# A tuned attention and SwiGLU kernel: units 12 to 15 by 15 products per three feature blocks, and silu as one activation

## Chip, cores and metric

The kernel runs on one core of a Trainium2 chip. Times are device microseconds of that core; the metric is the median of repeated executions. The core has a matmul engine (TensorE, "PE" in the profile, with its weight loads as "PEld"), VectorE (DVE), ScalarE (ACT), GpSimd (POOL) and a queue that issues transfers (SP). Each runs its own instructions in order, and semaphores tie them together.

## What is computed

Two stages, cut from the reference. The attention output of all tokens (4 batches of 768, 8 heads of 48) is reshaped to 3072 rows of 384 and goes through a gated feed-forward block with 1536 features:

```python
for t in range(S):
    cur = np.einsum('bhd,bhe->bhde', u[None] * kt, vt)
    y[:, :, t] = np.einsum('bhd,bhde->bhe', rt, state + cur)
    state = w[None, :, :, None] * state + np.einsum('bhd,bhe->bhde', kt, vt)
...
g = x @ w_gate
silu = g * (1.0 / (1.0 + np.exp(-g)))
val = x @ w_val
return (silu * val @ w_out)
```

## The kernel before

**Tiling.** Tokens are cut into 24 units of 128 (6 chunks of 4 batches). Attention makes, for unit i, a transposed input tile xT (384 rows in three blocks of 128, by 128 tokens). The feed-forward block works on groups g of two units (256 tokens), and from g = 2 on two groups at a time. Its 1536 features are 12 blocks of 128; each needs gate and value. All is fp32, so one 128x256 product shows as two matmul records in the profile.

**Three forms of the same products.** A plain group (`gate_value`, L444, units 0 to 3) takes 3 products for the gate and 3 for the value of a feature block. For a pair of groups (512 tokens) `four` (L590, units 4 to 15) makes a block's gate and value from 11 products in place of 12, with sums of weights made by POOL (`w_sums`, L576) and of inputs made by VectorE (`x_sums`). The names p1 to p7, c11 to c22 are its products; `PLACE` (L556) says at which step each is issued, and ACT and VectorE copy and add the partial sums out of two PSUM chains, a and b. Copies p1, u2 and u3 go to partial buffers (a ring of six). For units 16 to 23 `three_units` (L808) takes three feature blocks at once: 15 rounds r0 to r14 of two products each (gate and value), in six PSUM chains (n, y, l4, l5, l1, l2, l8), for 30 products in place of 33. The weight forms that they need are made by POOL, six sums in place (`in_place`, L707) and nine into side buffers (`w_forms`, L719), the input forms by VectorE (`x_forms`, L751, 11 operations).

**Silu.** ACT makes the sigmoid into a buffer; VectorE (or POOL) multiplies it by the gate, then by the value.

**Projection.** `project` (L501) makes a group's output rows from seven products of quarter matrices, with sums from `h_sums` (L486), ACT copies and VectorE additions. `two_projections` (L663) gives the order in which two groups' items run ("00 10 01 02 11 04 03 12 05 06 13 14 15 16": group, product), and hangs the preparation of the next pair onto them.

**PSUM.** Eight banks: four for attention (also used by `three_units`), two for gate_value and chain a, one each for the tags "o" and "w_mag".

**Order.** The order is written out by hand. Step s of the main loop prepares unit s+1 (POOL scales k and r, L301 and L304), runs scores of s-1 (L381), outputs and update of s-2 (L411, L426), turns blocks of unit s on VectorE (L373) and moves those of s+1 by 16 transfers on SP (L358). Between these parts `gaps` (L907) calls `feed`, which takes feed-forward pieces from the list `todo`; `queue(g)` (L886) fills it at every second step with the 26 pieces of `four_units` for one pair and the projection items of the pair before. When the attention is done, the pieces of `three_units` run for units 16 to 23 with their projections.

Of the kernel before, what the change touches and what calls it, by code (L numbers as in the profile page):

```python
# [22 lines left out]
def fast(  # L23
# [39 lines left out]
    six = ctx.enter_context(tc.tile_pool(name="six", bufs=6))  # L63
    ps_a = ctx.enter_context(tc.tile_pool(name="ps_a", bufs=4, space=bass.MemoryType.PSUM))
    ps_w = ctx.enter_context(tc.tile_pool(name="ps_w", bufs=1, space=bass.MemoryType.PSUM))
    ps_f = ctx.enter_context(tc.tile_pool(name="ps_f", bufs=2, space=bass.MemoryType.PSUM))
    ps_o = ctx.enter_context(tc.tile_pool(name="ps_o", bufs=1, space=bass.MemoryType.PSUM))
# [18 lines left out]
    hTs = cst.tile([P, 2, FC, 2 * P], FP32, name="hTs")  # L86
# [81 lines left out]
    def round_high(n, half, bank):  # L168
        hi = halves(bits[n][:, :, 1], n)[half]
        ps, tag = ((ps_w, "w_mag"), (ps_o, "o"))[bank]  # L170
        mag = ps.tile([P, WN // 2], INT32, name="w_mag", tag=tag)
        mags[n, half] = mag[:].rearrange("p (c f) -> p c f", c=hi.shape[1])
        act.activation(
            mags[n, half].bitcast(FP32), hi.bitcast(FP32), AF.Copy, scale=float(2.0**-112)
        )
# [82 lines left out]
    act.activation(sg0[:], ident[:, 0:1], AF.Sigmoid)  # L258
# [185 lines left out]
    def gate_value(g, f):  # L444
        gv = ps_f.tile([P, 2, 2 * P], FP32, name="gv", tag="gv")
        for o, wt in enumerate((wg, wv)):
            for c in range(CC):
                pe.matmul(  # L448
                    gv[:, o, :].rearrange("p (i t) -> p i t", i=2),
                    wt[:, c, P * f : P * (f + 1)], xT[:, 2 * g % NX : 2 * g % NX + 2, c, :],  # L450
                    start=(c == 0), stop=(c == CC - 1),
                )
        sg = three.tile([P, 2 * P], FP32, name="sg", tag="sg")
        act.activation(sg[:], gv[:, 0, :], AF.Sigmoid)
        dve.tensor_mul(sg[:], sg[:], gv[:, 0, :])
        dve.tensor_mul(hT[g][:, f, :], sg[:], gv[:, 1, :])
# [44 lines left out]
    def project(g, n):  # L501

        h11, h12, h21, h22 = h_quarters(g)
        x = part_of.setdefault(g, {})
        if n == 0:
            one_bank = ps_f.tile([P, 2, 2 * P], FP32, name="o_f", tag="gv")[:, 0, 0:NH]
            if g % 2 == 0:
                x["a"] = ps_o.tile([P, 2 * P], FP32, name="o_a", tag="o")[:, 0:NH]
                x["b"] = one_bank
            else:  # L510
                x["a"] = one_bank
                x["b"] = ps_w.tile([P, 2 * P], FP32, name="o_b", tag="w_mag")[:, 0:NH]
            x["out"] = [two.tile([P, DM], FP32, name=n, tag=n) for n in ("o_sb1", "o_sb2")]
        lhs, rhs, acc = (
            (h11, w11, "a"), (h12, w21, "b"), (1, wt[0], "a"), (2, wt[1], "a"),
            (0, w12, "b"), (h22, wt[2], "a"), (3, w22, "b"),
        )[n]
        if isinstance(lhs, int):
            lhs = x["s"][lhs]
        ps = x[acc]  # L520
        for f in range(FH):
            pe.matmul(  # L522
                ps, lhs[:, f, :], rhs[:, f, :],
                start=(f == 0 and n in (0, 1, 4)), stop=(f == FH - 1), skip_group_check=True,
            )
        o1, o2 = x["out"]
        if n in (0, 2, 3):
            nm = {0: "p1", 2: "u2", 3: "u3"}[n]
            x[nm] = six.tile([P, 2 * P], FP32, name=nm, tag="part")[:, 0:NH]
            act.copy(x[nm], ps)  # L530
        elif n == 1:
            dve.tensor_add(o1[:, 0:NH], x["p1"], ps)
        elif n == 5:
            act.copy(o2[:, 0:NH], ps)
        elif n == 6:
            dve.tensor_add(o1[:, NH:DM], x["u2"], ps)  # L536
        if n in (3, 4):
            if "c22" in x:
                dve.tensor_add(o2[:, NH:DM], x["u3"], x["b"])
            x["c22"] = True  # L540
        if n >= 5:
            j = 6 - n
            c, b = divmod(2 * g + j, B)
            n0 = S * b + P * c
            act.dma_start(out=out[n0 : n0 + P, :], in_=x["out"][j][:])
# [44 lines left out]
    def four(g, f, what):  # L590

        x = part_of[g]
        if what == "p1":
            x["a", f] = ps_f.tile([P, 2, 2 * P], FP32, name="c_a", tag="gv")[:, 0]
        elif what == "p2":
            pool_of, tag = ((ps_o, "o"), (ps_w, "w_mag"))[f % 2]
            x["b", f] = pool_of.tile([P, 2 * P], FP32, name="c_b", tag=tag)[:]
        h = [hT[g + j][:, f, :] for j in range(2)]
        if what in ("sg0", "sg1"):
            j = int(what[2])  # L600
            x[what, f] = three.tile([P, 2 * P], FP32, name="sg", tag="sg")
            act.activation(x[what, f][:], h[j], AF.Sigmoid)  # L602
            return
        if what == "h1":
            dve.tensor_mul(h[1], h[1], x.pop(("sg1", f))[:])  # L605
            pool.tensor_mul(h[1], h[1], x.pop(("u3", f))[:])  # L606
            return
# [13 lines left out]
        ps = x[acc, f]  # L621
# [4 lines left out]
        if what in ("p1", "p6", "p7"):  # L626
            nm = {"p1": "p1", "p6": "u2", "p7": "u3"}[what]
            x[nm, f] = six.tile([P, 2 * P], FP32, name=nm, tag="part")
            act.copy(x[nm, f][:], ps)  # L629
        elif what == "c11":  # L630
            dve.tensor_add(h[0], x.pop(("p1", f))[:], ps)  # L631
        elif what == "c21":
            dve.tensor_mul(h[0], h[0], x.pop(("sg0", f))[:])
            dve.tensor_mul(h[0], h[0], ps)
        elif what == "c22":
            dve.tensor_add(x["u3", f][:], x["u3", f][:], ps)  # L636
        elif what == "c12":
            dve.tensor_add(h[1], x.pop(("u2", f))[:], ps)

    def four_units(g):  # L640

        steps = sorted((11 * f - 5 + at, f, what) for f in range(FC) for what, at in PLACE.items())
        if g + 2 == THREES:
            steps += [
                (11 * f + 20 + 5.4 * m, f, do)
                for f in (2, 5, 8) for m, do in enumerate(in_place(f // 3))
            ]
            steps.sort(key=lambda x: x[0])
# [14 lines left out]
    def two_projections(g):  # L663

        def item(j, p):
            if g >= THREES and (j, p) == (0, 1):
# [6 lines left out]
            elif g + 2 < THREES:  # L673
# [4 lines left out]
            if THREES <= g + 2 < N // 2:  # L678
# [6 lines left out]
    THREES = 8  # L685
# [33 lines left out]
    def w_forms(t):  # L719

        f = 3 * t
        made = wide["u", t] = {}

        w = [[wgv[:, :, c, P * (f + i) : P * (f + i + 1)] for c in range(CC)] for i in range(3)]
        def place():
            if t == 0:
# [24 lines left out]
    def x_forms(g):  # L751
# [4 lines left out]
        v += [  # L756
            t[:].rearrange("p h d -> p (h d)")[:, 0 : 2 * P].rearrange("p (i t) -> p i t", i=2)
            for t in r_ld + k_ld
        ]
        last = two.tile([P, H, D], FP32, name="xf", tag="rk")  # L760
        v.append(
            last[:].rearrange("p h d -> p (h d)")[:, 0 : 2 * P].rearrange("p (i t) -> p i t", i=2)
        )
        v10, v14, v6, v13, v2, v12, d1, v3, v1, v8, v4 = v
        dve.tensor_add(v10, x01, x21)
        dve.tensor_add(v14, x10, x20)
# [8 lines left out]
        dve.tensor_sub(v4, x01, x00)  # L775
        wide["v", g] = {
# [4 lines left out]
    def prepare_threes(g, n):  # L781
        if g > THREES:
            if n == 10:
                x_forms(g)
            return
        if n == 1:
            todo_forms.extend(in_place(3) + w_forms(1))
        if n == 7:
            todo_forms.extendleft(reversed(w_forms(0)))
# [4 lines left out]
    def three_step(g, t, n):  # L794

        what, chain = ROUNDS[27 - n if t == 3 and n > 12 else n]
        first = n == [c for _, c in ROUNDS].index(chain)
        if first:
            pool_of, tag = {"l4": (ps_o, "o"), "l2": (ps_w, "w_mag")}.get(chain, (ps_a, "a"))
            wide[chain] = pool_of.tile([P, 2, 2 * P], FP32, name=f"c_{chain}", tag=tag)  # L800
        u, v = wide["u", t][what], wide["v", g][what]
        for o in range(2):
            pe.matmul(  # L803
                wide[chain][:, o].rearrange("p (i t) -> p i t", i=2), u[:, o], v,
                start=first and o == 0, stop=True, skip_group_check=True,
            )

    def three_units(g):  # L808
# [8 lines left out]
        def bank(chain):  # L817
            return wide[chain][:].rearrange("p o t -> p (o t)")
# [4 lines left out]
        def silu(at, n, which, h, on, muls):  # L823
            sg = room["sg"][n].rearrange("p (j t) -> p j t", j=2)
            gate, value = (which[:, :, o] for o in range(2))
            todo.append((at, lambda: act.activation(sg, gate, AF.Sigmoid)))  # L826
            todo.append((muls, lambda: on.tensor_mul(sg, sg, gate)))  # L827
            todo.append((muls + 0.1, lambda: on.tensor_mul(h, sg, value)))

        if g == THREES:  # L830
            forms = w_forms(2) + w_forms(3)
            todo += [(2.1 * n + 0.2, do) for n, do in enumerate(forms)]
        for t in range(4):
            z = 15 * t
            for n in range(15):
                todo.append((z + n, lambda t=t, n=n: three_step(g, t, n)))
# [6 lines left out]
            later(z + 6.5, dve.tensor_sub, c[4], q14, "l4")  # L843
            later(z + 8.5, act.copy, x, "n")
# [9 lines left out]
            later(z + r0, dve.tensor_sub, c[2], c[2], "l2")  # L854
            later(z + 11.6, dve.tensor_sub, c[0], r12, "n")
# [30 lines left out]
    def queue(g):  # L886
# [5 lines left out]
        elif g % 2 and g > 1:  # L892
# [5 lines left out]
            *pieces, last = four_units(g - 1)  # L898
# [111 lines left out]
    for s in range(4, N + 2):  # L1010
# [34 lines left out]
        if s == 24:  # L1045
            x_forms(THREES)
# [434 lines left out]
```

## Time and profile before

| | |
|---|---|
| median of 3 runs | 618.14 us (617.55 to 618.4) |
| profiled execution | 618.37 us, its span 616.6 us |
| granted TensorE clock | 0.999 |
| TensorE busy | 601.6 us, 98% of the span |
| VectorE, ACT, POOL busy | 395.5, 235.0, 325.4 us |
| units 12 to 15 beside attention | about 343 to 418 us of the span |
| units 16 to 23 | from 450.5 us on |

The span is from the first to the last instruction; the execution's own time has some 1.8 us around it. A group's row names line, engine, operation and tiles (out<-in), then count, busy time, mean duration, and the engine's idle time ahead of the group with what ended it. A matmul's end is modelled and matmuls overlap in the pipeline, so their starts are read, not their durations. Idle time of an engine that sets nothing costs nothing.

### The profile page before, as it was taken

What the parts mean: (1) busy time and instruction counts of PE and PEld (TensorE: products, weight loads), DVE (VectorE), ACT (ScalarE), POOL (GpSimd) and SP (SyncE); (2) the same over time, 40 slices, a digit from 0 to 9 for tenths busy, and PEclk for the clock granted to TensorE, in tenths of its full rate; (3) what the DMA queues carried; (4) which work ended last, traced back from release to release, by engine and by line L of the source; (5) the groups of instructions that cost most, each with busy time, mean ns of one, the idle gap of its engine ahead of it and who ended that gap; (6) DMA issues with size and microseconds to landing.
All of it is one profiled execution on the core that took longest, in us unless ns stands there. A gap on an engine that the chain in (4) does not pass through costs nothing.

```text
span 616.6 us, 12802 instructions
## 1 busy us (share of the span) xinstructions
PE 601.6 (98%) x4992; PEld 541.4 (88%) x4992; DVE 395.5 (64%) x749; ACT 235.0 (38%) x599; POOL 325.4 (53%) x366
## 2 busy tenths in 40 slices
PE   8799999999999999999999999999999999999996
PEld 7588888899888899988899988889978889988896
DVE  6878997464556564466659255649268885478770
ACT  3368886321343422244431334442223331133310
POOL 4789789944638422764624747959736510012200
PEclk9999999999999999999999999999999999999999
DMA  7979982342331213323231503031000000100001
GB/s 176 224 208 244 245 289 46 65 69 59 73 66 25 33 22 71 70 32 55 43 48 29 112 13 48 11 48 28 27 27 2 0 1 14 38 1 2 1 2 55
DMA packets 138005, 40.44 MB, mean 66 GB/s; under 512 B 128592, under 2 KB 131792, under 8 KB 137936
## 3 DMA queue, kind: packets, MB, share of 16 engines
q1 hardware_dynamic: 134480, 34.82, 26.6%
q10 hardware_dynamic: 3456, 4.72, 2.1%
q8 instruction: 41, 0.67, 0.5%
q14 instruction: 28, 0.23, 0.1%
HBM read 28.51 MB, written 4.72 MB: 54 GB/s over the span
## 4 chain that ended last, share of the span: by engine, by line
PE 83%; DMA 4%; SPq 3%; POOL 3%; DVE 3%; ACT 2%; issue 1%; ACTq 0%; DVEq 0%; POOLq 0%
PE o_f L522 13%; PE c_b L622 11%; PE c_l L803 10%; PE c_a L622 10%; PE gv L448 8%; PE o_a L522 8%; PE o_b L522 6%; PE y_ps L411 5%; PE c_y L803 3%; PE c_n L803 3%; PE s_ps L381 3%; SPq L358 3%; DMA w_bits<-in_moe_w_gate_dram 1%; DMA w_bits<-in_moe_w_val_dram 1%; PE u_ps L426 1%
## 5 line engine op out<-in xcount | busy, mean ns | idle before, releaser
L448 PE MATMUL gv<-xT,wgv 128*128 128x256 f32 x288 | 66.8, 385 | 0.6 <-ACT xT L415 0.6
L322 ACT ACTIVATE At<-ident,du 128x128 f32<-128x128 f32 x176 | 61.0, 397 | 15.8 <-DVE o_sb L536 7.2
L622 PE MATMUL c_b<-xT,wgv 128*128 128x256 f32 x216 | 64.4, 380 | 0.0
L827 POOL TENSOR_TENSOR At<-At,hats 128x512 f32<-128x512 f32 x8 | 10.2, 1274 | 97.8 <-ACT At L826 97.8
L448 PEld LDWEIGHTS gv<-xT,wgv 128*128 128x128 f32 x288 | 53.2, 190 | 8.9 <-ACT xT L415 0.9
L606 POOL TENSOR_TENSOR hTs<-hTs,u 128x256 f32<-128x256 f32 x36 | 28.5, 791 | 48.6 <-DVE hTs L605 48.4
L622 PEld LDWEIGHTS c_b<-xT,wgv 128*128 128x128 f32 x216 | 40.7, 190 | 5.3
L629 ACT COPY u<-c_a 128x256 f32<-128x256 f32 x72 | 26.7, 371 | 47.8 <-PE c_a L622 44.9
L386 DVE COPY_PREDICATED At<-mask,s_ps 128x512 f32<-128x512 int32 x48 | 33.0, 742 | 18.2 <-PE s_ps L381 9.7
L622 PE MATMUL c_a<-t,s 128*128 128x256 f32 x144 | 43.6, 384 | 0.7 <-ACT p L629 0.7
L622 PE MATMUL c_a<-xT,wgv 128*128 128x256 f32 x144 | 42.8, 379 | 0.0
L602 ACT ACTIVATE sg<-hTs 128x256 f32<-128x256 f32 x72 | 29.9, 416 | 28.8 <-DVE hTs L631 21.1
L304 POOL TENSOR_TENSOR hats<-r_ld,scales 128x384 f32<-128x384 f32 x20 | 21.2, 1061 | 33.0 <-DMA hats<-hats 33.0
L622 PE MATMUL c_b<-xT,s 128*128 128x256 f32 x144 | 37.0, 379 | 0.0
L636 DVE TENSOR_TENSOR u<-u,c_b 128x256 f32<-128x256 f32 x36 | 15.0, 417 | 33.3 <-PE c_b L622 29.6
L411 PE MATMUL y_ps<-At,v_ld 128*32 128x128 f32 x768 | 34.9, 273 | 1.4 <-DVE At L386 1.4
L411 PEld LDWEIGHTS y_ps<-At,v_ld 128*32 128x32 f32 x768 | 30.3, 110 | 2.4 <-issue 1.4
L622 PEld LDWEIGHTS c_a<-t,s 128*128 128x128 f32 x144 | 26.7, 190 | 5.1 <-ACT p L629 1.5
L622 PEld LDWEIGHTS c_b<-xT,s 128*128 128x128 f32 x144 | 27.2, 190 | 3.9
L622 PEld LDWEIGHTS c_a<-xT,wgv 128*128 128x128 f32 x144 | 27.3, 190 | 3.6
L439 POOL TENSOR_TENSOR Z<-Z,w 48x192 f32<-48x192 f32 x32 | 18.7, 583 | 22.2 <-DVE Z L438 21.0
L411 PE MATMUL y_ps<-rT,Z 112*32 112x128 f32 x480 | 29.8, 276 | 0.5 <-ACT kT L347 0.5
(240 smaller groups left out, 1524.0 us busy)
## 6 DMA issues: line engine op xcount, KB each, us to landing
hats<-hats SPq DMA_DIRECT2D x192, 32.0 KB, 2.0
w_bits<-in_moe_w_gate_dram SPq DMA_DIRECT2D x6, 768.0 KB, 6.2
v_ld<-in_v_dram SPq DMA_DIRECT2D x48, 96.0 KB, 3.3
w_bits<-in_moe_w_val_dram SPq DMA_DIRECT2D x6, 768.0 KB, 6.6
w_bits<-in_moe_w_out_dram SPq DMA_DIRECT2D x6, 768.0 KB, 6.6
out_dram<-o_sb ACTq DMA_DIRECT2D x24, 192.0 KB, 2.0
k_ld<-in_k_dram SPq DMA_DIRECT2D x20, 192.0 KB, 3.1
r_ld<-in_r_dram SPq DMA_DIRECT2D x20, 192.0 KB, 4.2
```

Of the source, the lines that this page charges most:

```text
L304: pool.tensor_mul(rhat_of(i)[:, :, 0:D], raw(i)[1], rscale)
L322: lambda h=h: act.activation(At[i % 2][:, h, :], ident[:], AF.Identity, scale=du[:, h : h + 1])
L386: dve.copy_predicated(At[i % 2][:].rearrange("p (a e) t -> p a e t", e=2)[:, :, e], mask[:].bitcast(INT32).unsqueeze(1).to_broadcast([P, H ...
L411: pe.matmul(ps[32 * q : 32 * q + 32, cc, :], *x, start=start, stop=stop, skip_group_check=True,)
L439: pool.tensor_mul(ze, ze, w)
L448: pe.matmul(gv[:, o, :].rearrange("p (i t) -> p i t", i=2), wt[:, c, P * f : P * (f + 1)], xT[:, 2 * g % NX : 2 * g % NX + 2, c, :], start ...
L522: pe.matmul(ps, lhs[:, f, :], rhs[:, f, :], start=(f == 0 and n in (0, 1, 4)), stop=(f == FH - 1), skip_group_check=True,)
L602: act.activation(x[what, f][:], h[j], AF.Sigmoid)
L606: pool.tensor_mul(h[1], h[1], x.pop(("u3", f))[:])
L622: pe.matmul(ps.rearrange("p (i t) -> p i t", i=2), lhs, rhs, start=first, stop=what not in ("p2", "p5", "p4", "p3"), skip_group_check=True,)
L629: act.copy(x[nm, f][:], ps)
L803: pe.matmul(wide[chain][:, o].rearrange("p (i t) -> p i t", i=2), u[:, o], v, start=first and o == 0, stop=True, skip_group_check=True,)
```

## The change

Units 12 to 15 (g = 6 and 7) are made by a new function `three_beside`, with the 15 rounds of `three_units`, while attention still runs. It has four PSUM banks in place of six chains' own tiles, so its rounds stand in another order (`BESIDE`, and `ENDING` for the last three blocks), and a bank goes back to a list as soon as its last reader is issued. The four banks that were three pools are now one list, `take()` and `free`, for all feed-forward work. Silu is one ACT activation, in place where it can be; the product with the gate goes away everywhere. Partial buffers come from the list `free_part`, and projections keep partial sums in the output tiles. `in_place` for the first nine blocks moves from beside units 12 to 15 to beside units 8 to 11. `x_forms` for units 16 to 19 moves from the end of step 24 to ahead of a projection item of units 12 to 15 (item "13": group 7, product 3).

```diff
+    banks = [ps_f.tile([P, 4 * P], FP32, name=f"bank{n}") for n in range(4)]
+    free = deque(banks[:2])
+    def take():
+        return free.popleft()
...
     def gate_value(g, f):
-        gv = ps_f.tile([P, 2, 2 * P], FP32, name="gv", tag="gv")
+        bank = take()
+        gv = bank[:].rearrange("p (o t) -> p o t", o=2)
...
-        act.activation(sg[:], gv[:, 0, :], AF.Sigmoid)
-        dve.tensor_mul(sg[:], sg[:], gv[:, 0, :])
-        dve.tensor_mul(hT[g][:, f, :], sg[:], gv[:, 1, :])
+        sg = free_sg.popleft()
+        act.activation(sg, gv[:, 0, :], AF.Silu)
+        dve.tensor_mul(hT[g][:, f, :], sg, gv[:, 1, :])
+        free_sg.append(sg)
+        free.append(bank)
...
     def project(g, n):
+            x["a"] = take()
...
+        if n == 1:
+            x["b"] = take()
...
         elif n == 5:
             act.copy(o2[:, 0:NH], ps)
+            free.append(x["a"])
...
     def four(g, f, what):
         if what in ("sg0", "sg1"):
-            act.activation(x[what, f][:], h[j], AF.Sigmoid)
+            act.activation(h[j], h[j], AF.Silu)
...
         if what in ("p1", "p6", "p7"):
-            x[nm, f] = six.tile([P, 2 * P], FP32, name=nm, tag="part")
-            act.copy(x[nm, f][:], ps)
+            x[nm, f] = free_part.popleft()
+            act.copy(x[nm, f], ps)
         elif what == "c11":
-            dve.tensor_add(h[0], x.pop(("p1", f))[:], ps)
+            free_part.appendleft(x.pop(("p1", f)))
+            dve.tensor_add(h[0], free_part[0], ps)
         elif what == "c21":
-            dve.tensor_mul(h[0], h[0], x.pop(("sg0", f))[:])
             dve.tensor_mul(h[0], h[0], ps)
+            free.append(x["a", f])
...
-    THREES = 8
+    FIRST, THREES = 6, 8
...
+    BESIDE = (
+        ("r10", "n"), ("r14", "y"), ("r12", "l4"), ("r13", "n"), ("r2", "y"), ("r9", "l4"),
+        ("r5", "n"), ("r11", "y"), ("r6", "l5"), ("r3", "l1"), ("r1", "l2"), ("r7", "l5"),
+        ("r4", "l1"), ("r0", "l2"), ("r8", "l8"),
+    )
...
+    def three_beside(g):
+        for t in range(4):
+            z = 15 * t
+            rounds = ENDING if t == 3 else BESIDE
...
+            if t < 3:
+                forms = w_forms(g, t + 1)
...
+            later(at["r10"], act.copy, c[5], "n")
+            later(at["r14"], act.copy, c[4], "y")
+            later(at["r12"], act.copy, c[0], "l4")
+            later(at["r13"], dve.tensor_add, c[4], c[4], "n")
+            later(at["r2"], dve.tensor_add, c[5], c[5], "y")
+            later(at["r9"], dve.tensor_sub, c[4], c[4], "l4")
+            give(at["r9"] + 0.1, "l4")
+            later(at["r5"], act.copy, c[1], "n")
+            later(at["r5"] + 0.1, dve.tensor_sub, c[0], c[0], "n")
+            give(at["r5"] + 0.2, "n")
+            later(at["r11"], act.copy, c[2], "y")
+            later(at["r11"] + 0.1, act.copy, c[3], "y")
+            give(at["r11"] + 0.2, "y")
...
+            later(at["r8"], dve.tensor_sub, c[1], c[1], "l8")
+            later(at["r8"] + 0.1, dve.tensor_add, c[3], c[3], "l8")
+            give(at["r8"] + 0.2, "l8")
+            if t < 3:
+                for i, on in enumerate((dve, dve, pool)):
+                    silu(
+                        *((z + 11.7, z + 11.8) if i == 2 else (z + 15.6 + i / 10, z + 16.2 + i / 10)),
+                        hTs[:, :, 3 * t + i], values[:, :, i], on,
+                    )
...
-            *pieces, last = four_units(g - 1)
+            *pieces, last = (four_units if g - 1 < FIRST else three_beside)(g - 1)
...
-        if s == 24:
-            x_forms(THREES)
```

Here `later(at, ...)` places an operation after the round that stands at that place, and `c` are six pairs of a gate row in hTs and a value buffer, all 128x512: c0 to c5 are the gate and value of three feature blocks for both groups.

## Prediction, made before the changed kernel ran

> **What bounds the kernel now.** I read the page's busy times first, then its chain of waits, then TensorE's instructions in order of time. From the page:
>
> ```profile
> span 616.6 us, 12802 instructions
> PE 601.6 (98%) x4992; PEld 541.4 (88%) x4992; DVE 395.5 (64%) x749; ACT 235.0 (38%) x599; POOL 325.4 (53%) x366
> PE 83%; DMA 4%; SPq 3%; POOL 3%; DVE 3%; ACT 2%; issue 1%; ACTq 0%; DVEq 0%; POOLq 0%
> L622 PE MATMUL c_b<-xT,wgv 128*128 128x256 f32 x216 | 64.4, 380 | 0.0
> ```
>
> TensorE is busy for 98% and carries 83% of the chain. Matmuls overlap in the records (380 ns each), so a product must be priced by its distance to the next one. TensorE in order of time, in the stage that changes (units 12 to 15), with columns start, duration, what, and the wait ahead of it:
>
> ```profile
> 350.70 0.59 PE L622 MATMUL c_b<-t,s 128*128 128x256 f32 x2
> 351.13 0.59 PE L622 MATMUL c_b<-xT,wgv 128*128 128x256 f32 x2
> 351.57 0.59 PE L622 MATMUL c_a<-xT,wgv 128*128 128x256 f32 x2
> 352.26 0.70 PE L622 MATMUL c_a<-t,wgv 128*128 128x256 f32 x2
> 352.80 0.59 PE L622 MATMUL c_a<-xT,wgv 128*128 128x256 f32 x2
> ```
>
> A product is two records (x2), and products start 0.432 us apart: nothing but their number sets the pace here. At 352.26 one is late by 0.26 us, and the next by another 0.11: a wait costs its length and some 0.11 for the restart. Two other places show such waits, at 303.41 and at the start of units 16 to 19:
>
> ```profile
> 303.41 0.70 PE L622 MATMUL c_a<-t,s 128*128 128x256 f32 x2 [0.38 <-ACT p L629]
> ...
> 452.35 1.03 PE L803 MATMUL c_l<-xf,wgv 128*128 128x256 f32 x4
> 454.47 1.10 PE L803 MATMUL c_l<-xf,wgv 128*128 128x256 f32 x4 [1.09 <-DVE xf L771]
> 455.41 1.03 PE L803 MATMUL c_n<-xf,s 128*128 128x256 f32 x4
> ```
>
> The stage's own windows row shows what is left on the other engines (us, busy us of PE, weight load, DVE, ACT, POOL):
>
> ```profile
> 343.00:418.00 75.00, 74.90 (x596) 66.02 (x595) 41.56 (x92) 31.54 (x90) 53.01 (x70) 1.00 0.24 42
> ```
>
> **What the Trainium skill says.** "ScalarE: Activation LUTs", Step-by-step: every function takes one element per cycle and lane, 0.833 ns each. The trace agrees: the sigmoid of 128x512 took 630 ns and the copy 587, so I price silu as sigmoid. The same page, Table sets, has a 2.66 us switch between sets, and puts copies into every set; the trace has one table load of 1.28 us, at 0.80 us, and the changed program also has one on its path, so I charge none. "SBUF — State Buffer", Who interferes with whom: a VectorE instruction with two SBUF inputs contends with GpSimd's reads, one with a PSUM input doesn't. The trace agrees: L633 (two SBUF inputs) took 653 ns in this stage where L634 (one in PSUM) took 422. So new additions from PSUM keep their price and new products of SBUF tiles may take more.
>
> **Part by part.** (1) Products. `four` is 11 per feature block: L622 has 792 records over three pairs, 132 products for a pair. The 15-product form is 15 rounds of 2 for three blocks: L803 has 480 records over two pairs, 120 for a pair. So 12 fewer x 0.432 = **-5.18 us**, all on TensorE, which is the path. Attention, projections and DMAs keep their counts; no queue gets or loses a transfer.
>
> (2) Waits that exist now. `x_forms(8)` moves from behind step 24 to ahead of projection item 13 of units 12 to 15. Its 11 subtractions (0.42 each, 4.6 us) then lie beside three more items of 1.95 us and attention: the wait at 454.47 goes, 452.35 to 454.47 being 2.12 instead of 0.86, with 0.08 at the restart: **-1.33**. Next late there would be POOL's forms for round r13, of which POOL has six in-place sums fewer (6 x 0.74) in that stretch. The wait at 352.26 goes with `four`: **-0.37**. The wait at 303.41 (0.64 with its restart) and one at 188.79 to 191.24 (0.91, the same line) came from `p1`'s copy queueing for a buffer that POOL's product L606 held. Partial buffers are now taken from the side last released, so `p1` takes one that VectorE gave back and the wait for POOL falls on the copy four products later. I count two thirds of 1.55: **-1.0**.
>
> (3) Silu. It takes the product of a gate with its sigmoid away 96 times (24 in `gate_value`, 48 in `four` for units 4 to 11, 24 in units 16 to 23, 8 of them on POOL), some 0.4 to 0.7 us each. TensorE waits for none of them in the views above, so: 0, hidden by TensorE's own stream; if that cover were gone it would be a gain.
>
> (4) POOL and ACT. The in-place weight sums of units 12 to 15 (18 x 0.74 = 13 us) move up beside units 8 to 11, where POOL is busy 44.2 of 78.0 us: it fits, and this mix with `four` ran at 53 of 75 here. In the changed stage POOL loses some 16 in-place sums, 28 L584-588 sums and 10 L606 (about 42 us) and gains 27 forms and three products of 1.27 (24 us). ACT has 24 copies of 0.587 and 11 silus, 21 us against 23. Each is covered by a 70 us stage: 0. Bounds: -0.5 to +1.0.
>
> (5) New waits in the stage. VectorE gets, for three blocks, 12 additions from PSUM at 0.686 (the L821 row) and two products, 9.6 us beside 15 rounds of 0.864 = 13.0; attention adds 4.1 us a unit (two L386, two transposes, a reduction, two L438) while TensorE's part of it takes 3.1 (390.30 to 393.41). It fits on average, not everywhere. A handover TensorE to ACT or VectorE takes 0.20 to 0.37 in units 16 to 19 (round start 472.69, copy 472.89), back 0.15 (454.32 to 454.47). With four banks and these, the written order gives four late places:
> - Third round (r12) takes the bank that projection item 15 has just left: 0.20 + copy 0.32 + 0.15 = 0.67 late. Behind it on TensorE is item 16, then everything.
> - First change of block, counted from its round r10 at 0: r8 is in c1 and c3 at 1.6; ACT does the n copy, two silus, then the y copy to 3.35, needed for r2 at 3.46: even. VectorE's two products end at 4.5, and behind them stand attention's two transposes (1.3), then the n addition, to 6.5. Round r5 wants to write that bank at 5.18: 1.45 late.
> - Second change: a diagonal ACTIVATE ahead of the y copy, 0.4 late at r2.
> - Third: transposes and reduction ahead of the products, 0.4 late at r2.
>
> Sum 2.9, with four restarts **+3.4**. Elsewhere a bank is reused two or three rounds (1.7 to 2.6 us) after its addition could start, 1.1 us of work: no wait. This is an unseen mixture, so bounds 0 and +8.
>
> Sum: -5.18 - 1.33 - 0.37 - 1.0 + 3.4 = **-4.5**. The profiled execution took 618.37 (its span 616.6 and 1.8 around it), 0.23 over the median of 618.14. That gives 613.9, or **613.7** against the median.
>
> **Rivals.** 0.2% (1.2 us) is what a measurement of this kernel can tell.
> - (A) The forecast, the saving less a few microseconds of waits: 611 to 616.8. Chance 0.64.
> - (B) The banks' slack holds and all waits vanish: -7.9, 610.3. For it: VectorE's back-to-back additions start 0.60 apart, not 0.69 (475.22, 475.82). Chance 0.16.
> - (C) The waits eat the saving: 7.9 us of them, 618. For it: r5, r2 and r9 each follow their copy by two rounds, with ACT also serving attention. Chance 0.11. That the fewer products are not the path belongs here; the 0.432 pitch speaks against it.
> - (D) Slower: VectorE becomes the bound at the bank handovers. If some twenty of the stage's 60 rounds wait 0.4 + 0.11, that is 10.7 us, 621. It decides from 9.1 us on. Against it: 41.6 of 75 us busy now, and 9.6 of 13.0 per three blocks plus attention still leaves a sixth. Chance 0.09.
>
> **How the numbers follow.** Faster by over 0.2% (under 616.9): A and B with a little taken off, 0.80. Same: 0.11. Slower: 0.09. The range reaches over most of B (down to 610.0) and the nearer half of C (up to 617.6); left out are 0.03 of B, 0.06 of C and D.
>
> **What would show it.** Right: 240 matmul records for units 12 to 15 and 528 for the other two pairs; no wait for xf at units 16 to 19; no wait on ACT p; waits of 0.4 to 1.5 us at r12, r5 and r2 of the new stage, ended by ACT copies and VectorE additions. Wrong: waits of over 5 us summed there, waits for POOL's forms, a second table load, a silu slower than 630 ns at 128x512, or gains before 340 us of over 2 us.

## The result, and the profile after

The changed kernel took **612.55 us** (median of 4 runs, 612.33 to 612.86) against 617.88 for the kernel before (the runs shown ahead of the prediction and one more): a ratio of 0.9913, 95% interval 0.9896 to 0.993. Measured again beside the last experiments it was 612.25 against 617.09, 0.992 (0.9907 to 0.9934). So it is faster by 4.8 to 5.3 us, where 4.5 was forecast. The page after:

```profile
span 610.8 us, 12619 instructions
PE 595.3 (97%) x4968; PEld 537.3 (88%) x4968; DVE 359.6 (59%) x652; ACT 233.0 (38%) x574; POOL 308.8 (51%) x355
PE 87%; POOL 2%; DVE 2%; ACT 1%; issue 1%; DMA 1%; SPq 0%; ACTq 0%; POOLq 0%
```

TensorE lost 24 records (4992 to 4968), the 12 products of two records each. VectorE lost 36 us, ACT 2, POOL 17: that is work beside the path, and the span went down by 5.8 us only.

TensorE's waits in the changed stage and behind it, in order of time (start, duration, what, and in brackets the wait with what ended it):

```profile
347.35 1.13 PE L817 MATMUL bank<-xf,wgv 128*128 128x256 f32 x4 [0.41 <-ACT o_sb L540]
...
369.90 1.99 PE L817 MATMUL bank<-xT,s 128*128 128x256 f32 x8 [0.63 <-DVE hv L842]
...
442.80 2.22 PE L530 MATMUL bank<-wo,hs 128*128 128x192 f32 x12 [1.19 <-DVE o_sb L546]
```

The first is round r12, which takes the bank that projection item 15 has left; the second is r5 at the first change of block. Both had been forecast. The third had not: it is projection item 16, behind the moved `x_forms`. The bracket counts only idle time; how late a start is comes from its distance to the start before, less the usual pitch: 0.57, 0.79 and 1.35 us, each with 0.10 more for the restart. A fourth wait, at r2 of the second change of block (381.3), is 0.12 and 0.10.

Why item 16 waits is seen on VectorE:

```profile
434.92 1.37 DVE L393 COPY_PREDICATED At<-mask,s_ps 128x512 f32<-128x512 int32 x2 [1.73 <-ACT At L329]
436.18 0.70 DVE L775 TENSOR_TENSOR xf<-xT 128x256 f32<-128x256 f32 x1
436.91 0.83 DVE L776 TENSOR_TENSOR xf<-xT,xf 128x256 f32<-128x256 f32 x1
...
442.06 0.42 DVE L785 TENSOR_TENSOR xf<-xT 128x256 f32<-128x256 f32 x1
442.40 0.35 DVE L546 TENSOR_TENSOR o_sb<-o_sb,bank 128x192 f32<-128x192 f32 x1
```

The 11 operations of `x_forms` run from 436.18 to 442.48. Behind them in VectorE's order stands L546, the addition that reads projection item 14's sum out of the bank into which item 16 adds. Item 14 started at 437.55 and item 15 behind it at 439.50, so the addition's input was there from about 439.7, and TensorE had item 16 to do from about 441.5.

**A ruler for the experiments.** TensorE's order of work is fixed by the program, and the noise of the start lies ahead of attention's scores near 157 us (TensorE's s_ps group). From those scores to the ones near 328 us the changed kernel and all that are built on it, the one with the other buffer order apart, took 171.15 us. The ruler is the distance from the scores near 157 us to the start of the last matmul record, in one profiled execution, worked out from TensorE's timeline:

| kernel | us | against the row it is built on |
|---|---|---|
| before | 454.17 | |
| before with silu only | 452.67 | -1.50 |
| 11-product form, new buffers, `x_forms` late | 451.81 | -0.86 |
| 15-product form, new buffers, `x_forms` late | 448.06 | -3.75 |
| the changed kernel | 448.18 | +0.12 |
| with `x_forms` at item 12 | 446.73 | -1.45 |
| with that, r12 behind item 16 and r13 earlier | 445.85 | -0.88 |
| with r2 earlier too | 445.15 | -0.70 |

A second profiled execution of the changed kernel gave 448.19. The first five rows add up to -5.99, which is 0.7 to 1.2 us more than the medians say. The row of silu holds a wait of 0.90 that need not belong to it (below); without it the sum is -5.09, between the two measurements. The medians come from more than one chip, on which the kernel before took 617.09 to 617.9, so two kernels are compared by their ratios to it or by the ruler.

### The profile page after: what moved, and what is told of

Same layout as the page of the kernel before. It is cut to its first block, busy times and chain, and to the rows that moved or that the text cites. A ratio compares the mean times of both kernels' runs of the same rounds, so it can differ in the third digit from the quotient of the medians.

```text
span 610.8 us, 12619 instructions
## 1 busy us (share of the span) xinstructions
PE 595.3 (97%) x4968; PEld 537.3 (88%) x4968; DVE 359.6 (59%) x652; ACT 233.0 (38%) x574; POOL 308.8 (51%) x355
## 4 chain that ended last, share of the span: by engine, by line
PE 87%; POOL 2%; DVE 2%; ACT 1%; issue 1%; DMA 1%; SPq 0%; ACTq 0%; POOLq 0%
PE bank L530 26%; PE bank L627 19%; PE bank L817 13%; PE bank L456 7%; PE c_l L817 6%; PE y_ps L418 5%; PE c_n L817 3%; PE c_y L817 3%; PE s_ps L388 3%; POOL wgv L223 1%; PE u_ps L433 1%; PE tp L350 1%; DMA r_ld<-in_r_dram 1%; ACT At L329 0%; POOL hats L311 0%
## 5 line engine op out<-in xcount | busy, mean ns | idle before, releaser
L456 PE MATMUL bank<-xT,wgv 128*128 128x256 f32 x288 | 66.8, 385 | 0.6 <-ACT xT L422 0.6
L627 PE MATMUL bank<-xT,wgv 128*128 128x256 f32 x240 | 64.3, 379 | 0.0
L456 PEld LDWEIGHTS bank<-xT,wgv 128*128 128x128 f32 x288 | 53.2, 190 | 8.9 <-ACT xT L422 0.8
L627 PEld LDWEIGHTS bank<-xT,wgv 128*128 128x128 f32 x240 | 45.4, 190 | 6.0
L530 PE MATMUL bank<-wo,hv 128*128 128x192 f32 x288 | 49.5, 327 | 0.0
L530 PEld LDWEIGHTS bank<-wo,hv 128*128 128x128 f32 x288 | 47.3, 190 | 0.5
L530 PE MATMUL bank<-wo,hs 128*128 128x192 f32 x240 | 42.4, 326 | 1.2 <-DVE o_sb L546 1.2
L530 PE MATMUL bank<-wt,hs 128*128 128x192 f32 x240 | 41.9, 327 | 0.0
L530 PEld LDWEIGHTS bank<-wo,hs 128*128 128x128 f32 x240 | 39.7, 190 | 1.8 <-DVE o_sb L546 1.5
L627 PE MATMUL bank<-t,s 128*128 128x256 f32 x144 | 39.8, 383 | 0.0
L530 PEld LDWEIGHTS bank<-wt,hs 128*128 128x128 f32 x240 | 39.3, 190 | 0.5 <-issue 0.4
L817 PE MATMUL bank<-xf,wgv 128*128 128x256 f32 x128 | 33.0, 381 | 0.4 <-ACT o_sb L540 0.4
```

The costliest lines, as they stand in the source:

```text
L456: pe.matmul(gv[:, o, :].rearrange("p (i t) -> p i t", i=2), wt[:, c, P * f : P * (f + 1)], xT[:, 2 * g % NX : 2 * g % NX + 2, c, :], start ...
L530: pe.matmul(ps, lhs[:, f, :], rhs[:, f, :], start=(f == 0 and n in (0, 1, 4)), stop=(f == FH - 1), skip_group_check=True,)
L627: pe.matmul(ps.rearrange("p (i t) -> p i t", i=2), lhs, rhs, start=first, stop=what not in ("p2", "p5", "p4", "p3"), skip_group_check=True,)
L817: pe.matmul(ps[:, o], u[:, o], v, start=first and o == 0, stop=True, skip_group_check=True,)
```

## The experiments

**Silu alone, on the kernel before.**

```diff
-            act.activation(x[what, f][:], h[j], AF.Sigmoid)
+            act.activation(h[j], h[j], AF.Silu)
...
-            dve.tensor_mul(h[0], h[0], x.pop(("sg0", f))[:])
             dve.tensor_mul(h[0], h[0], ps)
```

and likewise in `gate_value` and `three_units`.

> The kernel before with silu as one activation and without the product of gate and sigmoid; nothing else is changed. By the prediction's part 3 the products hide behind TensorE: 618 us, 0 against before. By the theory from the two traces they don't quite: in each of four projections of before, the sums hs stand on VectorE behind two products of a gate with its sigmoid, and TensorE starts the item 'wt,hs' 0.18 us late (0.07 and a restart of 0.10) at 228, 323, 509 and 589 us. Then these four go, -0.7 us, and 617.2; the wait for xf (1.33) stays. If the waits on ACT p (0.90 and 0.64) also came from the products, since POOL's product waits behind VectorE's, they go here too: 615.7.

Measured: 616.74 against 617.26, ratio 0.9992 (0.9983 to 1.0). TensorE's timeline at one of the four places, first of before, then with silu alone:

```profile
224.55 4.06 PE L522 MATMUL o_f<-wo,hTs 128*128 128x192 f32 x24
228.56 2.19 PE L522 MATMUL o_a<-wt,hs 128*128 128x192 f32 x12
```

```profile
223.51 4.06 PE L521 MATMUL o_f<-wo,hTs 128*128 128x192 f32 x24
227.41 2.11 PE L521 MATMUL o_a<-wt,hs 128*128 128x192 f32 x12
```

From the first start to the second it is 4.01 us, then 3.90, which is 24 records of 0.163; and the group behind the wait takes 2.19, then 2.11. That is 0.11 and 0.07 at each place, and all four are gone (0.71). The wait on ACT p near 302 grew from 0.64 to 0.86:

```profile
302.35 0.70 PE L619 MATMUL c_a<-t,s 128*128 128x256 f32 x2 [0.59 <-ACT p L626]
```

The wait of 0.90 near 189 is gone too, but that silu took it away is not shown. POOL's work there starts when attention's 16 transfers have landed. First of before, then with silu alone:

```profile
179.88 1.01 POOL L304 TENSOR_TENSOR hats<-r_ld,scales 128x384 f32<-128x384 f32 x1 [9.99 <-DMA hats<-hats]
```

```profile
178.21 1.00 POOL L304 TENSOR_TENSOR hats<-r_ld,scales 128x384 f32<-128x384 f32 x1 [10.68 <-DMA hats<-hats]
```

Counted from the scores near 157 this is 23.26 us, then 21.73, and in the twelve profiled executions of all kernels it lies between 21.73 and 23.66. SP had issued the transfers at the same distance in both (until 20.3 us). So POOL, which holds the buffer that the copy waits for, started 1.5 us earlier in this execution; how much of the 0.90 came from that is not known.

So silu is worth something: 1.5 us between two single executions, 0.6 of it without the wait near 189, and 0.5 (0 to 1.05) by the medians.

**The order of the free partial buffers.**

```diff
-            free_part.appendleft(x.pop(("p1", f)))
-            dve.tensor_add(h[0], free_part[0], ps)
+            free_part.append(x.pop(("p1", f)))
+            dve.tensor_add(h[0], free_part[-1], ps)
```

and the same for `u2`.

> The changed kernel with its partial buffers returned at the back of the free list (first released, first taken) in place of the front. By the prediction's part 2 the buffer order is what took the waits on ACT p away: they come back, 0.90 near 188 and 0.64 near 302 us, and the time is 614.1. By the rival silu took them away (POOL's product no longer queues behind one on VectorE): no such wait, 612.6.

Measured: 623.19 against 617.26, ratio 1.0097 (1.0082 to 1.0112), far above both numbers. POOL, then ACT, then TensorE in the timeline of this kernel:

```profile
179.61 0.99 POOL L311 TENSOR_TENSOR hats<-r_ld,scales 128x384 f32<-128x384 f32 x1 [11.88 <-DMA hats<-hats]
...
182.58 0.72 POOL L611 TENSOR_TENSOR hv<-hv 128x256 f32<-128x256 f32 x1
```

```profile
183.33 0.37 ACT L634 COPY hv<-bank 128x256 f32<-128x256 f32 x1 [7.58 <-POOL hv L611]
```

```profile
183.76 1.22 PE L627 MATMUL bank<-t,s 128*128 128x256 f32 x2 [6.43 <-ACT hv L634]
```

POOL waited 11.9 us for attention's 16 transfers, and its product L611 with the last partial sum queued behind. With the list in order of release, ACT's next copy drew just that product's buffer. In the changed kernel POOL waited 11.7 us at the same place, but a buffer that VectorE has given back lies in front, and the same copy of ACT did not wait for POOL:

```profile
176.47 0.37 ACT L634 COPY hv<-bank 128x256 f32<-128x256 f32 x1 [0.30 <-PE bank L627]
```

So the order of the list decides here. What came back were not the two waits of before, but others: 6.6 us at 177 with 3.1 more in the slow restart behind it, 1.3 at 307.9, again with ACT's copy waiting for POOL, and 0.9 at 311.2.

**The 11-product form back, all else kept.**

```diff
-    FIRST, THREES = 6, 8
+    FIRST, THREES = 8, 8
```

> The changed kernel with units 12 to 15 in the 11-product form again; silu, the buffer list and the moved x_forms stay. By the account of the traces the 15-product form is worth 5.18 us of products and 0.37 of a wait, less 1.79 of new waits: 3.8, so this takes 616.3. If the form's new waits cost more than the trace shows, less: 615. If fewer products are not what shortened the path, 612.6.

Measured: 619.09 against 617.26, ratio 1.0026 (1.0016 to 1.0036): slower than the kernel before, and none of the three numbers. The wait at projection item 16 was 3.35 us here. POOL had six in-place sums more to make here and was busy to 446.6 in place of 440.1, so nine of the 11 operations of `x_forms` took 0.71 to 0.94 us in place of five, 8.3 us together in place of 6.3. TensorE, and then a windows row for the 4 us behind the wait (the last three numbers are granted clock, DMA share and GB/s):

```profile
447.88 4.21 PE L530 MATMUL bank<-wo,hs 128*128 128x192 f32 x12 [3.19 <-DVE o_sb L546]
```

```profile
447.50:451.50 4.00, 3.62 (x11) 3.62 (x12) 0.33 (x2) 0.00 (x0) 0.00 (x0) 0.50 0.14 49
```

The twelve records took 4.21 us in place of 2.22. This run therefore prices a bad place for `x_forms`, not the product form.

**`x_forms` behind step 24 again, in before's order of operations.**

```diff
-        if g >= THREES and n == 10:
+        if g > THREES and n == 10:
             x_forms(g)
...
+        if s == 24:
+            x_forms(THREES)
```

> The changed kernel with x_forms for units 16 to 19 behind step 24 again, in before's order. By the theory that the move only exchanged one wait for another of its size, the wait of 1.35 and a restart on DVE o_sb at projection item 16 goes and the wait for xf of 1.25 comes back: 612.5, no change. By the prediction (the move takes a wait away and makes none): 613.9. If the additions run free of POOL here, since POOL has fewer forms to make beside them, the wait for xf comes back smaller or not at all: 611.2.

Measured: 612.02 against 617.26, ratio 0.9917 (0.9904 to 0.9931); the changed kernel's ratios are 0.9913 and 0.992. No difference can be told. L546 no longer delays item 16, and the old wait is back with its old size:

```profile
449.64 1.10 PE L820 MATMUL c_l<-xf,wgv 128*128 128x256 f32 x4 [1.09 <-DVE xf L782]
```

**The 11-product form with `x_forms` late**, the two edits above together, so that the form is priced free of the bad place.

> The changed kernel with units 12 to 15 in the 11-product form and x_forms behind step 24 again, so that the additions don't delay the projection's own: silu and the buffer list stay. By the account of the traces the 15-product form is worth 5.18 us of products and 0.37 of a wait, less 1.79 of new waits, 3.8: 612.0 of the changed kernel with x_forms late gives 615.8, with the wait of 0.26 at c_a (350 us) back and no waits of 0.57, 0.79 and 0.12 in the stage. By the rival that the moved x_forms hurt for another reason than VectorE's order: still near 619.

Measured: 616.13 against 617.9, ratio 0.9972 (0.9963 to 0.9981). Against the kernel with `x_forms` late, the 15-product form is worth 3.5 us by the medians, each taken against the kernel before on its own chip, and 3.75 by the ruler, where 3.8 had been worked out. The wait of 0.26 near 350 was there, the other three were not.

This kernel also shows what became of the wait on ACT p near 302. ACT's copy and POOL's product, first with silu alone, then here:

```profile
301.92 0.37 ACT L626 COPY p<-c_a 128x256 f32<-128x256 f32 x1 [1.98 <-POOL hTs L603]
301.16 0.73 POOL L603 TENSOR_TENSOR hTs<-hTs,u 128x256 f32<-128x256 f32 x1
```

```profile
300.89 0.37 ACT L634 COPY hv<-bank 128x256 f32<-128x256 f32 x1 [0.58 <-PE bank L627]
301.30 0.73 POOL L611 TENSOR_TENSOR hv<-hv 128x256 f32<-128x256 f32 x1
```

POOL's product comes no earlier, but the copy takes another buffer and is done before it; by the ruler this is the whole -0.86 of the row. Two things are new about the buffers, their order and that projections no longer draw from them. Which of the two moved this wait is not shown.

**`x_forms` three projection items earlier.**

```diff
-        if g >= THREES and n == 10:
+        if g >= THREES and n == (7 if g == THREES else 10):
```

> The changed kernel with x_forms for units 16 to 19 three projection items earlier (ahead of group 7's product 2, just behind the addition L546 near 428), where VectorE is idle for 4.6 us. If the wait at projection item 16 is VectorE's order alone, both waits go: 612.5 less 1.45 is 611.1. If the additions, beside POOL's, take 6.5 us or more and make the addition at 432.8 or the attention copy at 434.9 late for TensorE, the wait moves there: 612.0 to 612.6.

Measured: 611.33 against 617.9, ratio 0.9898 (0.9882 to 0.9914). VectorE:

```profile
427.93 0.35 DVE L546 TENSOR_TENSOR o_sb<-o_sb,bank 128x192 f32<-128x192 f32 x1
428.19 0.42 DVE L775 TENSOR_TENSOR xf<-xT 128x256 f32<-128x256 f32 x1
...
432.04 0.42 DVE L785 TENSOR_TENSOR xf<-xT 128x256 f32<-128x256 f32 x1
432.66 0.35 DVE L543 TENSOR_TENSOR o_sb<-o_sb,bank 128x192 f32<-128x192 f32 x1 [0.20 <-PE bank L530]
```

The 11 operations fit into an idle stretch and ran at 0.42 to 0.43 each, since POOL read nothing beside them. TensorE has no wait at item 16 and none for xf: 1.45 by the ruler.

**Round r13 of the second block one piece earlier.**

```diff
-            pieces[n if n < 3 else 3 + (n - 3) * 23 // 57] += q
+            pieces[n if n < 3 else 8 if n == 18 else 3 + (n - 3) * 23 // 57] += q
```

> The changed kernel with round r13 of the second block (and its addition on VectorE) one feed-forward piece earlier, so that the addition stands ahead of attention's two transposes instead of behind them. By the prediction's reading of the first change of block, the wait of 0.79 and its restart of 0.10 at r5 go: 611.7. If attention misses its transposes 0.7 us later, or the y addition comes late in its place at r11, as much comes back: 612.5.

Measured: 612.46 against 617.9, ratio 0.9922 (0.9896 to 0.9948): no gain can be told (0.2 by the ruler). r5 is on time; the wait went to the next round, r11:

```profile
370.71 1.10 PE L817 MATMUL bank<-xT,s 128*128 128x256 f32 x4 [0.44 <-DVE hv L842]
```

The n addition now stands ahead of the two transposes, but the y addition, which frees the bank for r11, is still behind them.

**Three edits together**, with r12 behind item 16:

```diff
-                others.insert(len(others) - 3 + k, pieces.pop(0))
+                others.insert(len(others) - 3 + k + (k == 2 and g - 1 == FIRST), pieces.pop(0))
```

> The two edits of the kernels with x_forms earlier and r13 earlier together, and round r12 of the first block behind projection item 16 in place of ahead of it, so that it doesn't take the bank that item 15 has just left. By the theory that each wait stands alone: less 1.45, 0.9 and 0.67, which is 609.5 of 612.5. If a wait that goes only bares the next one (POOL's weight forms, the ring of four banks): 610.5 to 611.5.

Measured: 610.71 against 617.9, ratio 0.9876 (0.9858 to 0.9894). The waits at r12 and at item 16 are gone, the one at r11 (0.61) is not.

**And r2 one piece earlier**, `n in (18, 19)` in the line for `pieces`:

> The kernel with all three edits, with round r2 and its addition also one piece earlier, so that both additions (banks of r5 and r11) stand ahead of attention's transposes. By the theory that the wait only went from r5 to r11, because the second addition still stood behind the transposes, it goes for good here: 0.61 and 0.08 less than with three edits, and no wait over 0.2 in the stage: about 609.9. If it goes one further (r9's subtraction behind the transposes, then the bank of r3): 610.7.

> The changed kernel as it is, on the same chip as the kernel with more edits: 612.5, with the waits of 0.57, 0.79, 0.12 and 1.35 at the same places.

Measured on the same chip: **609.11** against 617.09, ratio 0.9867 (0.9851 to 0.9882), and the changed kernel 612.25 (ratio above). The waits of the changed kernel were at their places again, 0.57, 0.80, 0.12 and 1.35. VectorE's order at the first change of block in the changed kernel, where the first of three additions frees the bank of r5, and then with the four edits, where both additions run ahead of the transposes:

```profile
366.19 1.86 DVE L842 TENSOR_TENSOR hv<-hv 128x512 f32<-128x512 f32 x2 [0.78 <-ACT hv L849]
367.98 0.70 DVE L380 STREAM_TRANSPOSE kT<-hats 128x512 f32<-128x512 f32 x1
368.61 0.66 DVE L380 STREAM_TRANSPOSE rT<-hats 128x512 f32<-128x512 f32 x1
369.20 1.84 DVE L842 TENSOR_TENSOR hv<-hv,bank 128x512 f32<-128x512 f32 x3
```

```profile
365.29 1.86 DVE L842 TENSOR_TENSOR hv<-hv 128x512 f32<-128x512 f32 x2 [0.78 <-ACT hv L849]
367.08 1.27 DVE L842 TENSOR_TENSOR hv<-hv,bank 128x512 f32<-128x512 f32 x2
368.27 0.70 DVE L380 STREAM_TRANSPOSE kT<-hats 128x512 f32<-128x512 f32 x1
```

With them TensorE has no wait over 0.12 left from 330 us on. This version beats both kernels: 3.1 us less than the changed one.

## Why the prediction was right, step by step

The time lay within the range and 1.15 us below the forecast. The mechanism was right: fewer products on the engine that sets the pace, less some waits at the handover of banks. Several terms of the sum were not. By steps:

**(1) Products, -5.18: right.** Less the new waits and with the wait of 0.37 at 352.26, the form came to 3.75 by the ruler against 3.76 from the records (5.18 + 0.37 - 1.79).

**(2) Waits that exist now: the sum of this step was near, two of its terms were not.** "The wait at 454.47 goes" held, but not -1.33 for it: what would be late next was looked for among POOL's forms, and it was VectorE's own order, L546 behind `x_forms`. That gave 1.45 back, and the move is worth +0.12 in place of -1.33. The step failed by asking who waits for the moved operations and not what is queued behind them on their engine. The p waits were worth 1.54 in the two traces, not 1.0. The one near 302 (0.64) went with the new buffers: it stays with silu alone and is absent in the kernel with the new buffers and the 11-product form. What took the one near 189 (0.90) away stays open: it went with silu alone, in an execution in which the transfers had landed early, and it is also absent with the new buffers where they landed late (23.66 us).

**(3) Silu, 0: wrong by 0.7 by the ruler, the p waits apart (0.5 by the medians, which don't exclude 0).** "TensorE waits for none of them" rested on views in which a wait of 0.11 and its restart don't stand out. The four late starts of a projection item were there, at 228, 323, 509 and 589 us. The silu price itself was right:

```profile
L849 ACT ACTIVATE hv<-hv 128x512 f32<-128x512 f32 x9 | 5.4, 630 | 6.3 <-DVE hv L842 6.3
L849 ACT ACTIVATE hv<-hv 128x768 f32<-128x768 f32 x2 | 1.7, 845 | 7.6 <-DVE hv L842 7.6
```

Silu of 128x512 took 630 ns, as the sigmoid of that shape, and the longer row took 215 ns for 256 elements more, 0.84 each. This agrees with what the prediction took from the Trainium skill's "ScalarE: Activation LUTs", Step-by-step, that a function's price is its elements. There is one table load in the trace, so the switch of 2.66 us, which that page has under "What ACT_TABLE_LOAD costs" and not under "Table sets", was not paid.

**(4) POOL and ACT, 0: held** for the changed kernel. POOL's load in the stage was mis-sized, though: it fell from 53.0 us to 46.6 (338.5 to 412.5 us of the span), not by the 18 that losing 42 and gaining 24 would give, mostly because 39 weight forms (L749) fell into the stretch and not 27. TensorE waited for none of these forms in the stage. The kernel with the 11-product form shows what POOL's load can cost elsewhere: beside six sums more, `x_forms` made TensorE wait 3.35 us in place of 1.35.

**(5) New waits, +3.4: measured 1.79.** Without the restarts, r12 was forecast 0.67 late and was 0.57. r5 was forecast 1.45 late and was 0.79. With r10 of the second block at 363.93, the transposes started 4.05 us after it, where 4.5 had been worked out, and the operations behind followed one another by 0.59 to 0.63 us, so r5 started 5.97 us after r10 and not 6.63. r2 was 0.12 late at the second change in place of 0.4, and not late at the third: there ACT's y copy started at 396.96 and r2's turn was at 397.70, with no diagonal ACTIVATE of attention between the silus and the copy, as there was one at the second change (380.42).

So that the forecast came out this close is luck: errors of opposite sign met. The wait for xf was only moved (1.45 too much gain); the new waits were priced 1.6 too dear, and silu's gain 0.5 to 0.7 too low. Whether the gain of p was too low as well hangs on the wait near 189. Of rival B, all waits gone at 610.3, this is the part that was missing: 0.67, 0.89, 0.22 and 1.45 us of waits at four places, and with three of them taken away by moving instructions the kernel reached 609.11. The forms of C and D, waits of 8 us and more in the stage, were not there.

## What to carry to other kernels

A moved instruction is to be costed at both ends: who waited for it, and what now stands behind it in its engine's order. Where buffers or banks go back to a list, the order of the list can decide whether the next taker meets the slowest reader. A wait that is gone from one profiled execution is not yet the work of an edit, when it hangs on transfers whose landing differs from one execution to the next. And in a kernel that is bound by one engine, its starts are worth scanning at the size of a restart (0.10 us here): four waits of 0.11 and their restarts cost as much as one that stood out.

## What the runs showed that had not been expected

Waits of TensorE up to 1.35 us cost their length and 0.07 to 0.10. The two longer ones, with idle times of 3.19 and 6.43 us in brackets above, were followed by a granted clock of 0.50 (447.5 to 451.5 and 183 to 188 us), with records at twice their distance (0.320 in place of 0.163 us in the projection, 0.427 in place of 0.216 in the feed-forward products). "TensorE: Matmul & The Clock Gate", Part 1, in the Trainium skill tells of such a state after an idle window of about 3.4 us. These runs agree roughly: the shorter of the two is a little under that, and a wait of 1.23 us in the second of these runs had no such state behind it. So the wait of 3.35 us cost about 2.9 us more after it: by the ruler that kernel took 456.71 us, and the same with `x_forms` late 451.81, of which 1.33 are its wait for xf with the restart; 456.71 - 450.48 is 6.2.

VectorE's `x_forms` took 0.42 to 0.43 us each where POOL was idle and 0.83 to 0.94 beside POOL's sums, one placement against the other: the place alone doubled their price. The Trainium skill's "SBUF — State Buffer", Who interferes with whom, names such a contention where both operands of VectorE's instruction lie in SBUF, as here; the size of it is measured here.
